# Four small products on the quarters of the matrix engine, in linear attention before a gated MLP

## The chip, the cores and the metric

The program runs on one core of a Trainium2 chip. The metric is the device time of one execution in microseconds (us). Five engines take part: PE (TensorE, the matrix engine; its weight loads are shown as PEld), DVE (VectorE), ACT (ScalarE), POOL (GpSimd) and SP (SyncE, which here only issues DMAs; ACT issues some in the first microseconds).

## The reference, cut to what matters

Inputs are q, k and v of 8 batches x 8 heads x 576 positions x 64, and two weight matrices of 512 x 2048 and 2048 x 512. The weights arrive in 64-bit floats, the rest in 32-bit floats.

```python
q_s = softmax(q, axis=-1)                 # over the 64 of a head
k_s = softmax(k, axis=2)                  # over the 576 positions
kv  = einsum('bhsd,bhse->bhde', k_s, v)   # one 64 x 64 matrix per head
x   = einsum('bhsd,bhde->bhse', q_s, kv)  # then (batch*position) x 512
h   = x @ w_in
out = (h * cos(h)) @ w_out
```

## The kernel before, in words

Positions: of the 576 of a batch, 512 are worked on with that batch, and the last 64 of every batch are collected through `x_left` in DRAM into a ninth block of 512 rows. There are thus nine blocks of 512 rows for the MLP.

The MLP. The 2048 middle columns are cut into 16 slices of 128. A unit is one slice of one block: four matrix products into a bank `h` (L1073 or L1081), the gate h*cos(h) on ACT and DVE (L1106 to L1121), and four products into four banks `acc` (L1159 or L1166). In the first units the operands stay plain 32-bit (L1073, L1159); later each operand is split into a high and a low part and three products in a faster format stand for one (L1081, L1166). Blocks 0 and 1 are taken in turn by eight slices each, then blocks 2 to 4, and the last four blocks in two pairs that share products (L1453). Weights are turned from 64-bit to 32-bit floats by two steps of ACT and two of DVE each (L556, L561, L567, L578).

Attention for one batch. Heads are taken in pairs p of neighbours, 2p and 2p+1, because two heads of 64 fill 128 partitions. `k_exps` does the softmax of k on DVE, POOL and ACT. `k_steps` multiplies k by v (L760): for each pair ten products, five chunks of positions for two heads, one head to the upper and one to the lower 64 partitions of the output bank, so each uses a half of PE's columns; then `kv_f32` (L783) copies the two 64 x 64 results onto the diagonal of a 128 x 128 matrix `kvw` which POOL has filled with zeros (L778). `q_steps` does the softmax of q. For batch 0's first two pairs (`alone`) its exponentials go row by row on ACT (L821), eighteen instructions with their sums, in two parts. `x_steps` brings q to head-dimension-first form: in batches 0 and 1 by PE transposes (L902, L906), in the later ones by DVE block transposes and a trip through DRAM (`q_rows`). Then `x_mm` (L923) multiplies, for one pair, the 128 x 128 matrix by q in two halves of 288 positions, into two banks. ACT copies 512 of the 576 positions as high part (L933) and the other 64 as rows for `x_left` (L936); DVE makes the low part. In batch 0 the copy is plain (`x_whole`), and ACT does all of it.

A 32-bit product is two records on PE in the profile (two weight loads, two MATMULs).

PSUM has eight banks: two `h`, four `acc`, two `att`. The attention takes `att` in turn after the start.

The order. Each step is added to a `Plan` with its engine, a cost, what it reads and writes and a due time (`CFG` holds the numbers that set these); the list `ORDER` then gives the order in which all steps are issued. An engine works through its own steps in that order and waits at each for what it needs. PE also gets products of zeros (`warm_up` L1647, `fill` L736) in the start.

The first loads are listed in `CFG["seq"]`: q, k and v of batch 0 by pairs of heads (two DMAs each), with the first weights among them, on the queues of SP and ACT.

Of the kernel before, what the change touches and what calls it, by code (L numbers as in the profile page):

```python
# [29 lines left out]
    XV=(),  # L30
    early=1,
# [4 lines left out]
    fill_kv=((0, 0), (0, 1), (0, 2), (0, 3)),  # L36
# [5 lines left out]
    t0=33.71,  # L42
    unit=5.32,
    att0=dict(k=(-11.28, 5.44), kv=(18.78, -0.31), q=(5.83, 11.45), qt=(12.05, 4.95), x=(9.45, -8.71)),
# [3 lines left out]
    bus=dict(k=1.15, q=1.4, v=1.2, i=2.0, o=1.32),  # L48
    slow=1.3,
# [312 lines left out]
def linear_attention_then_cos_gated_mlp(  # L362
# [58 lines left out]
    def v_parts(t):  # L421
        return (
            t[:, 0 : CM * WV].rearrange("p (x w) -> p x w", w=WV),
            t[:, CM * WV : VW].rearrange("p (h w) -> p h w", w=WL),
        )
# [228 lines left out]
    def load_v(b, p, due, seq=(), eng="SP"):  # L654
# [21 lines left out]
        if own:  # L676
            plan.add("DVE", 0.45, frame, writes=place, due=due)
# [1054 lines left out]
```

## Time and profile before

| | |
|---|---|
| time, median of 3 runs | 872.33 us (871.9 to 872.65) |
| the profiled execution, span from its first to its last instruction | 871.6 us |
| median time less that span | 0.7 us |
| mean granted TensorE clock | 0.991 |
| PE, PEld, DVE, ACT, POOL busy | 98%, 79%, 70%, 61%, 9% |

The profile is of one execution. The granted clock is a share of full speed: 1.00 is the 2.4 GHz level, 0.50 the 1.2 GHz level. In a timeline row "x40" is the number of records merged, and a duration ends with the last record's own modelled end, so the time that a run of records takes from its neighbours is read from start to start.

### The profile page before, as it was taken

The page shows a single profiled execution, that of the slowest core. Times are in us where ns is not written, and L with a number is a line of the kernel's source. Part 1 is how long each engine was busy: PE and PEld are TensorE (multiplying, and loading weights), DVE is VectorE, ACT ScalarE, POOL GpSimd, SP SyncE. Part 2 cuts the span into 40 slices and gives each one's busy share as a digit, 9 for nine tenths or more (in the row PEclk, how much of TensorE's full clock was granted, in tenths as well). Part 3 has the DMA queues.
Part 4 walks back from the last instruction along what each step waited for, and adds up shares of the span by engine and source line. Part 5 has one row for each costly group of instructions (what it writes and reads, how often), then busy time and mean ns, then how long its engine had stood idle before and what let it go on. Part 6 is the DMA issues. An engine that isn't in the chain of part 4 may idle for free.

```text
span 871.6 us, 12196 instructions
## 1 busy us (share of the span) xinstructions
PE 855.9 (98%) x4224; PEld 687.8 (79%) x4224; DVE 605.7 (70%) x976; ACT 533.3 (61%) x913; POOL 76.6 (9%) x149
## 2 busy tenths in 40 slices
PE   6999999999999999999999999999999999999997
PEld 5754678888888888888888888888888888888886
DVE  5799899987676676585698988774547736454542
ACT  5898898646555656755774776664546635353441
POOL 1110100010001001001001002111100201111000
PEclk8899999999999999999999999999999999999999
DMA  9945495237943442463478727875423726243123
GB/s 232 341 118 157 152 261 170 78 77 232 285 128 98 103 105 72 106 155 104 126 195 261 229 86 209 213 205 159 135 85 109 215 78 193 85 151 91 37 54 91
DMA packets 151996, 130.30 MB, mean 150 GB/s; under 512 B 65920, under 2 KB 125312, under 8 KB 151936
## 3 DMA queue, kind: packets, MB, share of 16 engines
q1 hardware_dynamic: 136208, 98.24, 39.8%
q0 software_dynamic: 13312, 29.36, 11.9%
q10 hardware_dynamic: 2416, 1.93, 0.8%
q8 instruction: 33, 0.54, 0.3%
q14 instruction: 27, 0.22, 0.1%
HBM read 89.92 MB, written 39.58 MB: 149 GB/s over the span
## 4 chain that ended last, share of the span: by engine, by line
PE 96%; DMA 1%; DVE 1%; SPq 1%; ACT 0%; issue 0%
PE acc L1166 43%; PE h L1081 22%; PE z L1453 10%; PE a L1453 8%; PE x L923 4%; PE h L1073 3%; PE acc L1159 2%; PE kv L760 2%; DMA q<-in_q_dram 1%; PE qt L736 1%; DMA raw_o<-in_moe_w_out_dram 1%; PE acc L736 0%; PE qt L902 0%; PE kv L736 0%; SPq L647 0%; DVE k L713 0%
## 5 line engine op out<-in xcount | busy, mean ns | idle before, releaser
L1081 PE MATMUL h<-x,w_i 128*128 128x512 f32 x864 | 208.8, 392 | 1.3 <-DVE kt L1121 1.3
L1081 PEld LDWEIGHTS h<-x,w_i 128*128 128x128 f32 x864 | 162.0, 188 | 36.0 <-DVE kt L1121 1.5
L1166 PE MATMUL acc<-w_o,ghi 128*128 128x512 f32 x592 | 188.5, 399 | 0.0
L1166 PEld LDWEIGHTS acc<-w_o,ghi 128*128 128x128 f32 x592 | 110.6, 188 | 24.3
L1166 PE MATMUL acc<-w_o,glo 128*128 128x512 f32 x296 | 115.6, 391 | 0.0
L1453 PE MATMUL z<-xs,s 128*128 128x512 f32 x384 | 96.7, 391 | 0.0
L1106 ACT ACTIVATE kt<-h 128x512 int32<-128x512 f32 x80 | 47.6, 596 | 75.6 <-PE h L1081 72.1
L1453 PEld LDWEIGHTS z<-xs,s 128*128 128x128 f32 x384 | 72.1, 188 | 15.2
L1110 DVE SCALAR_TENSOR_TENSOR kt<-kt,h 128x512 f32<-128x512 int32 x80 | 54.7, 684 | 40.1 <-ACT kt L1106 39.9
L1453 PE MATMUL a<-xs,s 128*128 128x512 f32 x288 | 73.4, 390 | 0.0
L1137 ACT CAST ghi<-kt 128x512 fp32r<-128x512 f32 x74 | 45.6, 620 | 38.9 <-PE acc L1166 33.6
L1166 PEld LDWEIGHTS acc<-w_o,glo 128*128 128x128 f32 x296 | 55.5, 188 | 11.9
L1453 PEld LDWEIGHTS a<-xs,s 128*128 128x128 f32 x288 | 54.0, 188 | 11.3
L1121 DVE TENSOR_TENSOR kt<-kt,h 128x512 f32<-128x512 f32 x74 | 50.4, 680 | 16.8 <-ACT kt L1116 16.3
L1116 ACT ACTIVATE kt<-kt 128x512 f32<-128x512 f32 x80 | 50.6, 632 | 16.6 <-DVE kt L1110 16.0
L1141 DVE TENSOR_TENSOR glo<-kt,ghi 128x512 fp32r<-128x512 f32 x74 | 50.6, 688 | 14.0 <-ACT ghi L1137 13.5
L1474 DVE TENSOR_TENSOR c<-a,c 128x512 f32<-128x512 f32 x32 | 22.1, 691 | 26.8 <-PE a L1453 19.5
L923 PE MATMUL x<-qf,kvw 128*128 128x288 f32 x128 | 38.6, 407 | 0.0
L1427 POOL DMA_DIRECT2D s<-w_sums x32 | 20.2, 630 | 168.1 <-PE a L1453 116.3
L1116 ACT ACT_TABLE_LOAD x27 | 34.6, 1283 | 0.5
L706 POOL PARTITION_ALL_REDUCE m<-m x32 | 24.8, 809 | 77.8 <-DVE m L700 69.0
L1467 ACT COPY c<-z 128x512 f32<-128x512 f32 x32 | 18.8, 586 | 19.9 <-PE z L1453 19.7
(638 smaller groups left out, 1474.4 us busy)
## 6 DMA issues: line engine op xcount, KB each, us to landing
s<-w_sums POOLq DMA_DIRECT2D x32, 512.0 KB, 4.1
q<-in_q_dram SPq DMA_DIRECT2D x32, 256.0 KB, 3.9
raw_o<-in_moe_w_out_dram SPq DMA_DIRECT2D x16, 512.0 KB, 7.1
s<-w_own POOLq DMA_DIRECT2D x16, 512.0 KB, 4.5
raw_i<-in_moe_w_in_dram SPq DMA_DIRECT2D x15, 512.0 KB, 6.4
v_sb<-in_v_dram SPq DMA_DIRECT2D x29, 256.0 KB, 3.6
k<-in_k_dram SPq DMA_DIRECT2D x14, 512.0 KB, 4.6
qf<-q_rows SPq DMA_DIRECT2D x24, 288.0 KB, 3.6
```

What stands on the lines that cost most here:

```text
L706: nc.gpsimd.partition_all_reduce(T["m", b, p0][:, hs].rearrange("p h d -> p (h d)"), T["m1", b, p0][:, hs].rearrange("p h d -> p (h d)"), ...
L923: nc.tensor.matmul(t[:, 0:HALF], T["kv", b, p], T["qf", b, p][:, cs], start=True, stop=True)
L1073: nc.tensor.matmul(o, T["wc", "i", f][:, 0, cs], T["whole"][:, c], start=(c == 0), stop=(c == KC - 1),)
L1081: nc.tensor.matmul(o, a, x, start=(c == 0 and n == 0), stop=(c == KC - 1 and n == 2))
L1106: nc.scalar.activation(t.bitcast(I32), src(), AF.Identity, bias=0.25, scale=1.0 / TWO_PI)
L1110: nc.vector.scalar_tensor_tensor(t, t.bitcast(I32), -TWO_PI, src(), op0=ALU.mult, op1=ALU.add)
L1116: nc.scalar.activation(t, t, AF.Sin, bias=0.5 * math.pi)
L1121: nc.vector.tensor_mul(o, t, src())
L1137: nc.scalar.copy(t, T["g", u])
L1141: nc.vector.tensor_sub(t, T["g", u], T["gh", u].bitcast(F32))
L1166: nc.tensor.matmul(T["acc", j], a[:, js], w, start=(first and n == 0), stop=(last and n == 2))
L1453: nc.tensor.matmul(o, a, x, start=(first and c == 0 and m == 0), stop=(c == 1 and m == 2), skip_group_check=not first,)
```

## The change

Heads are paired two apart: of the four heads 4a to 4a+3, pair 2a+i holds heads 4a+i and 4a+i+2 (h = 0 and 1). The kv results are kept as 128 x 64 (head h on partitions 64h to 64h+63) with no zeros around them and one copy per pair (L783's two become one; POOL's memset goes). x of two pairs is four products of 64 x 64 weights by 512 positions, each with 64 rows and 64 columns of PE of its own, into two banks that then hold two heads each; the leftover 64 positions of all four pairs are kept apart (`ql`, `q_left`) and are eight products of 64 positions in two further banks, with one row store per batch. In batch 0 the four copies of x are shared between ACT and DVE (`XV=(1, 3)`).

The first loads of k, q and v go by four heads (k one DMA of 512 KB and one of 64 KB; q four DMAs; v two, or four where the two standing tiles take it). In batch 0 the k steps go by four heads as in the other batches, and the first maximum of q is one instruction over all rows. `early` goes from 1 to 2: the first two units' products wait for each quarter of x by itself. Two products of zeros less (`fill_kv`). All due times of the start, load costs and the whole `ORDER` are new.

The core of the diff (the order list, load helpers, the q rows in DRAM and renamings are left out):

```diff
-    XV=(),
-    early=1,
+    XV=(1, 3),
+    early=2,
...
-    fill_kv=((0, 0), (0, 1), (0, 2), (0, 3)),
+    fill_kv=((0, 0), (0, 1)),
...
     seq=[
-        ("q", 0, "SP"), ("k", 0, "ACT"), ("q", 1, "SP"), ("i", 0, "ACT"), ("k", 1, "ACT"), ("v", 0, "SP"),
-        ("q", 2, "SP"), ("v", 1, "ACT"), ("q", 3, "SP"), ("k", 2, "SP"), ("k", 3, "SP"), ("v", 2, "SP"), ("v", 3, "SP"),
-        ("i", 1, "SP"), ("o", 0, "SP"),
+        ("k", 0, "SP"), ("q", 0, "ACT"), ("v", 0, "SP"), ("k", 1, "ACT"), ("i", 0, "SP"), ("q", 1, "SP"),
+        ("v", 1, "SP"), ("i", 1, "SP"), ("o", 0, "SP"),
     ],
...
+    def pair_of(x, b, a, i):
+        return x[b].rearrange("(a h i) s d -> a i h s d", h=2, i=2)[a, i]
...
                         nc.tensor.matmul(
-                            x[h * D : (h + 1) * D, a : a + vt.shape[1]], t[:, h, c, :], vt,
+                            x[h * D : (h + 1) * D, to : to + vt.shape[1]], t[:, i + 2 * h, c, :], vt,
                             start=(c == CM), stop=(c == CM - 1),
                         )
...
         def kv_f32(i):
-            for h in range(2):
-                rows = slice(h * D, (h + 1) * D)
-                nc.scalar.activation(
-                    T["kv", b, ps_[i]][rows, rows], T["kvp", b, ps_[0]][rows, 2 * P * i + 1 : 2 * P * i + D + 1],
-                    AF.Copy, scale=T["r", b, ps_[0]][rows, i : i + 1],
-                )
+            t = T["kv", b, 2 * a + i] = sbt([P, D], F32, kvws[i], f"kvw_{b}_{2 * a + i}")
+            nc.scalar.activation(
+                t, T["kvp", b, a][:, 2 * P * i + 1 : 2 * P * i + D + 1], AF.Copy, scale=T["r", b, a][:, i : i + 1],
+            )
...
-        def x_mm(i):
-            t = T["xp", b, p, i] = bank(xo[i], f"x{i}_{b}_{p}")
-            cs = slice(i * HALF, (i + 1) * HALF)
-            nc.tensor.matmul(t[:, 0:HALF], T["kv", b, p], T["qf", b, p][:, cs], start=True, stop=True)
...
+        def quarters_of(banks, cols, moving, a):
+            for h, i in ((0, 0), (1, 1), (0, 1), (1, 0)):
+                rows, to = slice(h * D, (h + 1) * D), slice(i * D, (i + 1) * D)
+                nc.tensor.matmul(
+                    banks[h][to, cols], T["kv", b, 2 * a + i][rows], moving(2 * a + i)[rows], start=True, stop=True,
+                )
+
+        def x_mm(a, xo):
+            banks = [bank(o, f"x_{b}_{2 * a + h}") for h, o in enumerate(xo)]
+            for h in range(2):
+                T["xp", b, 2 * a + h] = banks[h]
+            quarters_of(banks, slice(0, NM), lambda p: T["qf", b, p], a)
+
+        def x_mm_left(xo):
+            banks = T["xlp", b] = [bank(o, f"xl{h}_{b}") for h, o in enumerate(xo)]
+            for a in range(2):
+                quarters_of(banks, slice(a * NL, (a + 1) * NL), lambda p: T["ql", b][:, p], a)
...
+        def x_hi(c, slot, own):
...
+            t = T["whole"][:, c] if whole else T["x", b, c][:, 0]
+            (nc.vector.tensor_copy if own else nc.scalar.copy)(t, T["xp", b, c])
```

The new list begins, for the engines that the prediction follows, with these steps of batch 0 (read off the list by counting the steps in the order in which they are added). PE: products of zeros and `warm_up`, k times v of heads 0 to 3, the transposes of pairs 1 and 0, zeros, `x_mm` of the first four heads, k times v of heads 4 to 7, zeros, the transposes of pair 2, of the leftover and of pair 3, zeros, the first product of unit 0, `x_mm` of the last four heads, the second product, the leftover products, and the other products of units 0 and 1 in turn. ACT: the DMAs of q and k, eighteen row exponentials of q, the exponential of k (heads 0 to 3), two weight steps, the copies of pairs 1 and 0, the exponential of q (pairs 2, 3), the kv copies, the exponential of k (heads 4 to 7), the copy of x. DVE: the maximum of q, the maxima of k, then the sums' reciprocals, the subtractions and products of both in turn.

## Rows read from the trace of the kernel before

**Rows 1.** Page, part 1: busy us (share of the span) x instructions.

```profile
PE 855.9 (98%) x4224; PEld 687.8 (79%) x4224; DVE 605.7 (70%) x976; ACT 533.3 (61%) x913; POOL 76.6 (9%) x149
```

**Rows 2.** Windows: each engine's busy us by stretch, then PEclk, DMA share, GB/s.

```profile
0.00:10.00 10.00, 7.76 (x29) 6.59 (x30) 3.97 (x30) 3.52 (x15) 2.27 (x12) 1.00 0.84 201
...
20.00:35.00 15.00, 14.34 (x119) 12.88 (x120) 13.85 (x32) 12.63 (x32) 2.55 (x5) 0.69 1.10 335
35.00:40.00 5.00, 5.00 (x25) 3.56 (x24) 1.38 (x2) 4.13 (x12) 0.71 (x3) 1.00 1.10 335
40.00:60.00 20.00, 20.00 (x102) 10.84 (x101) 19.02 (x32) 19.34 (x32) 3.26 (x4) 1.00 0.60 181
60.00:80.00 20.00, 20.00 (x92) 10.01 (x91) 18.18 (x27) 17.77 (x33) 0.20 (x1) 1.00 0.38 99
80.00:100.00 20.00, 20.00 (x66) 11.25 (x65) 18.31 (x32) 17.86 (x35) 2.40 (x6) 1.00 0.54 158
100.00:112.00 12.00, 11.75 (x119) 9.37 (x117) 10.95 (x20) 11.64 (x19) 1.59 (x3) 1.00 0.70 204
112.00:150.00 38.00, 36.92 (x163) 30.54 (x164) 35.56 (x48) 35.18 (x51) 0.31 (x1) 1.00 0.80 231
...
200.00:560.00 360.00, 360.00 (x1912) 295.32 (x1911) 263.38 (x423) 227.82 (x366) 27.63 (x56) 1.00 0.58 160
```

**Rows 3.** Timeline of PE: start us, us, operation, records [idle before, releaser].

```profile
15.72 1.35 PE L760 MATMUL kv<-v_sb,k 128*64 128x66 f32 x20 [3.36 <-issue]
20.00 1.36 PE L760 MATMUL kv<-v_sb,k 128*64 128x66 f32 x20 [2.92 <-ACT k L719]
...
34.74 1.02 PE L1073 MATMUL h<-x_whole,room_i 128*128 128x512 f32 x2
...
39.73 1.02 PE L1073 MATMUL h<-x_whole,room_i 128*128 128x512 f32 x2
...
113.08 3.01 PE L1081 MATMUL h<-x,w_i 128*128 128x512 f32 x12 [1.33 <-DVE kt L1121]
```

**Rows 4.** Timeline of PE: records of x and of plain 32-bit products.

```profile
80.13 3.60 PE L1073 MATMUL h<-x_whole,room_i 128*128 128x512 f32 x8
83.56 1.13 PE L923 MATMUL x<-qf,kvw 128*128 128x288 f32 x4
84.53 3.60 PE L1159 MATMUL acc<-room_o,g 128*128 128x512 f32 x8
```

**Rows 5.** Timeline of PE: one k-times-v step and its neighbours.

```profile
204.14 1.99 PE L1081 MATMUL h<-x,w_i 128*128 128x512 f32 x8
206.06 1.39 PE L760 MATMUL kv<-v_sb,k 128*64 128x66 f32 x40
207.37 0.73 PE L1166 MATMUL acc<-w_o,ghi 128*128 128x512 f32 x2
207.94 0.39 PE L1166 MATMUL acc<-w_o,glo 128*128 128x512 f32 x1
208.17 0.62 PE L1166 MATMUL acc<-w_o,ghi 128*128 128x512 f32 x2
208.64 0.40 PE L1166 MATMUL acc<-w_o,glo 128*128 128x512 f32 x1
```

**Rows 6.** Lines of ACT by shape: count | busy us, mean ns | idle before, releaser.

```profile
L783 ACT ACTIVATE kvw<-kv,r 64x64 f32<-64x64 f32 x64 | 19.6, 307 | 4.0 <-DVE r L774 3.3
...
L719 ACT ACTIVATE k<-k 128x1280 f32<-128x1280 f32 x14 | 17.8, 1275 | 0.1
L851 ACT ACTIVATE q<-q 128x1152 f32<-128x1152 f32 x15 | 17.5, 1167 | 0.1
...
L821 ACT ACTIVATE q<-q,qm 128x64 f32<-128x64 f32 x18 | 6.0, 336 | 0.0
```

**Rows 7.** Timeline of DVE in the start.

```profile
5.77 0.69 DVE L842 TENSOR_REDUCE qm<-q 128x8 f32<-128x512 f32 x1 [2.09 <-DMA q<-in_q_dram]
...
17.09 1.35 DVE L837 TENSOR_REDUCE qm<-q 128x18 f32<-128x1152 f32 x1 [3.08 <-ACT q L821]
```

More of the change, by code (lines that the diff above doesn't have):

```diff
@@ L434, in v_frame @@
         return t
-    NV = 2
-    v_sb = [v_frame(vp.tile([P, VW], F32, name=f"v_sb{i}")) for i in range(NV)]
+    v_sb = [v_frame(vp.tile([P, VW], F32, name=f"v_sb{i}"), 2) for i in range(2)]
     w_in = w_in.bitcast(U32)
@@ L654, in load_v @@
-    def load_v(b, p, due, seq=(), eng="SP"):
-        q_of = nc.scalar if eng == "ACT" else nc.sync
-        own = b == 0 and p >= NV
-        slot = ring("x4k") if own else None
-        place = quarters(slot) if own else [("v", p % NV)]
-        def frame():
-            T["v", b, p] = v_frame(sbt([P, VW], F32, slot, f"v_{b}_{p}"))
-        def load():
-            t = T["v", b, p] if own else v_sb[p % NV]
-            main, last = v_parts(t)
-            src = v[b, 2 * p : 2 * p + 2]
+        plan.add("POOL" if b else "DVE", 0.31, frame, writes=places, due=due)
@@ new lines, in load_k, with load_q @@
+        plan.load(CFG["bus"]["k"] * 2, load, writes=places, due=due, parts=2, eng=eng)
+        return places
+    def load_q(b, a, place, due, eng="SP"):
+        places = place if isinstance(place, list) else [(place, i) for i in (0, 1)]
+        tag = place if not isinstance(place, list) else spot(*place[0][1:])
+        def load():
+            t = T["q", b, a] = sbt([P, 9, P], F32, tag, f"q_{b}_{a}")
+            q_of = QUEUE[eng]
+            for i in range(2):
+                s2 = pair_of(q, b, a, i)
+                q_of.dma_start(
+                    t[:, NC * i : NC * i + CM, :].rearrange("p c (h d) -> p c h d", h=2),
+                    s2[:, 0:NM, :].rearrange("h (p c) d -> p c h d", c=CM),
+                )
+                q_of.dma_start(
+                    t[NL * i : NL * (i + 1), CM, :].rearrange("p (h d) -> p h d", h=2),
+                    s2[:, NM:S, :].rearrange("h p d -> p h d"),
+                )
+        plan.load(CFG["bus"]["q"] * 2, load, writes=places, due=due, parts=4, eng=eng)
+        return places
@@ L788, in k_steps @@
-        if (b, ps_[0]) in CFG["fill_kv"]:
-            fill(o, 3, ("fill", b, ps_[0]), f"kv_{b}_{ps_[0]}", o, due_kv)
-        plan.add("PE", 0.93 if n == 1 else 1.51, kv, reads=kr + vr, writes=[o], due=due_kv)
-        plan.add("DVE", 0.41 if n == 1 else 0.62, kv_inv, reads=[o], writes=[r])
-        for i in range(n):
-            plan.add("POOL", 0.14, lambda i=i: kv_frame(i), writes=[kvws[i]], due=due_kv)
-            plan.add("ACT", 0.62, lambda i=i: kv_f32(i), reads=[o, r], writes=[kvws[i]])
@@ L799, in q_steps @@
+        plan.add("DVE", 0.62, kv_inv, reads=[o], writes=[r])
+        for i in range(2):
+            plan.add("ACT", 0.31, lambda i=i: kv_f32(i), reads=[o, r], writes=[kvws[i]])
+        return kvws
+    def q_steps(b, a, qr, due):
         qm, qs = ring("qm"), ring("qs")
-        def rows():
-            return T["q", b, a].rearrange("p c (h d) -> p c h d", h=2)
-        def over_d(m):
-            return m.rearrange("p c (h o) -> p c h o", o=1).broadcast_to([P, 9, 2, D])
-        parts = ((0, 2 * CM), (2 * CM, 4 * CM + 2))
@@ L816, in q_exps, with q_exp @@
+        def q_exp():
+            t = T["q", b, a]
+            nc.scalar.activation(t, t, AF.Exp)
         def q_exps(i):
-            if i == 0:
-                T["qs", b, a] = sbt([P, 9, 2], F32, qs, f"qs_{b}_{a}")
-            t, m, o = rows_of(i), flat(T["qm", b, a], i), flat(T["qs", b, a], i)
-            for r in range(parts[i][1] - parts[i][0]):
+            t, m, o = heads(T["q", b, a]), T["qm", b, a], T["qs", b, a]
+            for r in range(parts[i].start, parts[i].stop):
                 nc.scalar.activation(
@@ L849, in q_exp, with q_norm @@
[L849 to L863 removed]
+        def q_norm(rs=slice(0, n)):
+            t = heads(T["q", b, a])[:, rs]
+            nc.vector.tensor_mul(t, t, over_d(T["qs", b, a], rs))
@@ L865, in q_steps @@
+        plan.add("DVE", 1.35, q_max, reads=qr, writes=[qm, qs] if alone else [qm], due=due)
         if alone:
-            done = [qr[:1], qr]
-            for i, n in ((0, 8), (1, 10)):
+            for i, rs in enumerate(parts):
+                m = rs.stop - rs.start
                 plan.add(
-                    "DVE", 0.07 * n + 0.1, lambda i=i: q_maxs(i), reads=done[i], writes=[(qm, i)] + [qm] * (1 - i), due=due
+                    "ACT", 0.335 * m, lambda i=i: q_exps(i), reads=[qm, qs], writes=[qr[i], (qs, i)], table="exp",
@@ L870, in q_steps @@
                 )
-                plan.add(
-                    "ACT", 0.335 * n, lambda i=i: q_exps(i), reads=[(qm, i)], writes=[*done[i], (qs, i)], table="exp"
-                )
-                plan.add("DVE", 0.42, lambda i=i: q_invs(i), reads=done[i], writes=[(qs, i)])
-                plan.add("DVE", 0.07 * n + 0.06, lambda i=i: q_norms(i), reads=[(qs, i)], writes=done[i])
+                plan.add("DVE", 0.42, lambda rs=rs: q_inv(rs), reads=[qr[i], qs], writes=[(qs, i)])
+                plan.add("DVE", 0.07 * m + 0.06, lambda rs=rs: q_norm(rs), reads=[(qs, i), qs], writes=[qr[i]])
@@ L876, in q_steps @@
             return
-        plan.add("DVE", 1.35, q_max, reads=qr, writes=[qm], due=due)
         plan.add("DVE", 1.35, q_sub, reads=[qm], writes=qr)
@@ L1007, in x_steps @@
-        if blocks:
-            qb = ring("qb")
-            old = [("x_left", i) for i in range(CFG["QD"] * NP)] if b == CFG["QD"] and p == 0 else []
-            plan.add("DVE", 0.71 if odd else 0.92, q_blocks, reads=qr, writes=[qb, *old], due=due_q)
-            qd, ql = [("qd", odd)], [("qd", odd, "left")]
-            left = [] if odd else [("qd", i, "left") for i in range(2)]
-            plan.load(1.05 if odd else 1.45, q_out, reads=[qb], writes=qd + left, parts=4 if odd else 8)
-            plan.load(0.95, q_in, reads=qd + ql, writes=[qf])
-        else:
-            if (b, p) in CFG["fill_q"]:
-                fill(o1, 4, ("fill", "q", b, p), f"qt1_{b}_{p}", o1, due_q)
-            plan.add(
-                "PE", 0.44 if odd else 0.55, q_tr, writes=[o1] if odd else [o1, o2],
-                reads=qr,
-                due=due_q,
-            )
-            if not odd:
-                plan.add("ACT", 0.23, q_side, reads=[o2], writes=[ring("ql")])
-            plan.add("ACT", 0.82, q_f32, reads=[o1, o2], writes=[qf])
@@ L1026, in x_steps @@
-        us = 0.49
-        for i in range(2):
-            plan.add("PE", us, lambda i=i: x_mm(i), reads=[qf, kvw], writes=[xo[i]], due=due_x)
-        if not keep:
-            for i in range(2):
-                plan.add("ACT", 0.4, lambda i=i: x_row(i), reads=[xo[i]], writes=[xs])
-            plan.load(0.9, put, reads=[xs], writes=[("x_main", p, b), ("x_left", p, b)], parts=2)
-            return []
-        for i, us in ((0, 0.4), (1, 0.58)):
-            xw = [("whole", p)] if whole else xr if i == 0 else xr[2:3]
-            plan.add("DVE" if own else "ACT", us, lambda i=i: x_hi(i), reads=[xo[i]], writes=xw + [xs] * i)
-            if not whole:
-                plan.add(
-                    "DVE", (0.45, 0.38)[i], lambda i=i: x_lo(i), reads=[xo[i], xr[2 * i]],
-                    writes=[xr[2 * i + 1]],
-                )
@@ new lines, in x_left_row, with put_left @@
+        def x_left_row(h):
+            if h == 0:
+                T["xl", b] = sbt([P, NP, NL], F32, xl, f"xl_{b}")
+            nc.scalar.copy(
+                T["xl", b][:, h::2], T["xlp", b][h][:, 0:P].rearrange("p (a n) -> p a n", a=2)
+            )
+        def put_left():
+            nc.sync.dma_start(
+                x_left[:, :, b * NL : (b + 1) * NL].rearrange("c p n -> p c n"), T["xl", b]
+            )
+        def x_hi(c, slot, own):
+            if whole and "whole" not in T:
+                T["whole"] = sbt([P, NP, TB], F32, "wi10", "x_whole")
+            if not whole:
+                T["x", b, c] = sbt([P, 2, TB], F32R, slot, f"x_{b}_{c}")
+            t = T["whole"][:, c] if whole else T["x", b, c][:, 0]
+            (nc.vector.tensor_copy if own else nc.scalar.copy)(t, T["xp", b, c])
@@ new lines, in x_lo, with late_hi, late_lo, late @@
+        def x_lo(c):
+            t = T["x", b, c]
+            nc.vector.tensor_sub(t[:, 1], T["xp", b, c], t[:, 0].bitcast(F32))
+        def late_hi(c, slot):
+            t = T["x", b, c] = sbt([P, 2, TB], F32R, slot, f"x_{b}_{c}")
+            nc.scalar.copy(t[:, 0], T["whole"][:, c])
+        def late_lo(c):
+            t = T["x", b, c]
+            nc.vector.tensor_sub(t[:, 1], T["whole"][:, c], t[:, 0].bitcast(F32))
+        def late(c, slot, xr):
+            plan.add("ACT", 0.62, lambda: late_hi(c, slot), reads=[("whole", c)], writes=[xr[0], xr[2]])
+            plan.add("DVE", 0.69, lambda: late_lo(c), reads=[("whole", c), xr[0]], writes=[xr[1], xr[3]])
@@ new lines, in x_row, with put @@
+        def x_row(c, xs):
+            T["xs", b, c] = sbt([P, TB], F32, xs, f"xs_{b}_{c}")
+            nc.scalar.copy(T["xs", b, c], T["xp", b, c])
+        def put(c):
+            nc.sync.dma_start(x_main[b, c], T["xs", b, c])
+        got = []
+        for a in range(2):
+            qfs = []
+            for i in range(2):
+                p = 2 * a + i
+                if blocks:
+                    qb, qf = ring("qb"), ring("row")
+                    plan.add(
+                        "DVE", 0.71 if i else 0.92, lambda p=p, qb=qb: q_blocks(p, qb), reads=qrs[a], writes=[qb],
+                        due=due_q(p),
+                    )
+                    plan.load(
+                        1.05 if i else 1.45, lambda p=p: q_out(p), reads=[qb],
+                        writes=[("qd", i)] + ([] if i else [("qdl", a)]), parts=4 if i else 8,
+                    )
+                    plan.load(0.85, lambda p=p, qf=qf: q_in(p, qf), reads=[("qd", i)], writes=[qf])
+                else:
+                    o, qf = ring(tq), ring("row")
+                    if (b, p) in CFG["fill_q"]:
+                        fill(o, 4, ("fill", "q", b, p), f"qt_{b}_{p}", o, due_q(p))
+                    plan.add("PE", 0.44, lambda p=p, o=o: q_tr(p, o), reads=qrs[a], writes=[o], due=due_q(p))
+                    plan.add("ACT", 0.59, lambda p=p, qf=qf: q_f32(p, qf), reads=[o], writes=[qf])
+                qfs.append(qf)
+            xo = [ring(tx), ring(tx)]
+            plan.add(
+                "PE", 1.15, lambda a=a, xo=xo: x_mm(a, xo), reads=[*qfs, kvw[2 * a], kvw[2 * a + 1]], writes=xo,
+                due=due_x(2 * a),
+            )
+            for h in range(2):
+                c = 2 * a + h
+                if not keep:
+                    xs = ring("row")
+                    plan.add("ACT", 0.59, lambda c=c, xs=xs: x_row(c, xs), reads=[xo[h]], writes=[xs])
+                    plan.load(0.73, lambda c=c: put(c), reads=[xs], writes=[("x_main", c, b)])
+                    continue
+                slot = ring("x4k")
+                xr = quarters(slot)
+                got += xr
+                own = whole and c in CFG["XV"]
+                xw = [("whole", c)] if whole else [xr[0], xr[2]]
+                plan.add(
+                    "DVE" if own else "ACT", 0.65 if own else 0.6, lambda c=c, slot=slot, own=own: x_hi(c, slot, own),
+                    reads=[xo[h]], writes=xw,
+                )
+                if whole:
+                    splits["x", c] = lambda c=c, slot=slot, xr=xr: late(c, slot, xr)
+                else:
+                    plan.add("DVE", 0.69, lambda c=c: x_lo(c), reads=[xo[h], xr[0]], writes=[xr[1], xr[3]])
@@ new lines, in x_steps @@
+        if blocks:
+            plan.load(0.5, q_in_left, reads=[("qdl", 0), ("qdl", 1)], writes=[ql])
+        else:
+            o = ring("att")
+            plan.add("PE", 0.25, lambda: q_tr_left(o), reads=qrs[0] + qrs[1], writes=[o], due=due_q(3))
+            plan.add("ACT", 0.35, q_left_f32, reads=[o], writes=[ql])
+        xo = [ring("att"), ring("att")]
+        plan.add("PE", 0.52, lambda: x_mm_left(xo), reads=[ql, *kvw.values()], writes=xo, due=due_x(3))
+        for h in range(2):
+            plan.add("ACT", 0.28, lambda h=h: x_left_row(h), reads=[xo[h]], writes=[xl])
@@ L1051, in linear_attention_then_cos_gated_mlp @@
+        plan.load(0.5, put_left, reads=[xl], writes=[("x_left", p, b) for p in range(NP)])
+        return got
     FH = CFG["FH"]
```

407 lines of the change are left out of this document (156 added, 251 removed), and 293 rows, old and new, of the table ORDER.

## The prediction

> **What bounds the kernel now.** I read the page's busy shares first: PE is busy for 98% of the span, DVE for 70%, ACT for 61% [rows 1]. A share over the whole span hides stages, so the windows come next. From 200 to 560 us PE is busy for all of the 360 us while DVE works 263 and ACT 228 [rows 2]: here a microsecond less on PE is a microsecond less in the end, and nothing else is near. The start is another matter. The timeline of PE has idle stretches of 3.36 and 2.92 us ahead of the first two k-times-v steps; the first product of unit 0 begins at 34.74 us and its third, which needs the third quarter of x, only at 39.73 [rows 3]. Between 20 and 112 us DVE works 13.85 + 1.38 + 19.02 + 18.18 + 18.31 + 10.95 = 81.7 of 92 us and ACT 83.4 [rows 2], and just behind that PE waits 1.33 us for DVE [rows 3]. So there are three stages: a start bound by the chain from loads through ACT and DVE, a stretch to about 150 us in which PE, DVE and ACT are all nearly full (112 to 150 us: 36.9, 35.6 and 35.2 of 38), and the rest, bound by PE.
>
> **The change on PE, batches 1 to 7.** Removed: eight products of 288 columns per batch. Two of them take 84.53 - 83.56 = 0.97 us from start to start [rows 4], 0.485 each, 3.88 us per batch. A record of 288 columns is then 0.2425 us, 0.842 ns per column; a record of 512 columns is (83.56 - 80.13) / 8 = 0.429 us [rows 4].
>
> Added: two groups of four products of 512 columns (8 records, 3.43 us if they ran one by one) and one group of eight products of 64 columns (16 records, 0.86 us). No row of before has products with 64 rows of their own. The nearest is k times v, where two products have 64 columns of PE each. I take its step between full-width neighbours [rows 5]: eight records from 204.14 at 0.23 us (the step from 207.94 to 208.17) end at 205.98; the step starts at 206.06; the next work starts at 207.37, and its first two records take 0.57 us instead of 0.47 (208.17 to 208.64). That makes 0.08 + 1.31 + 0.10 = 1.49 us. Its 40 records of 65 columns would be 2.19 us one by one and 1.09 us two abreast. Thus two products do run side by side, and going to small products and back costs about 0.40 us.
>
> With four abreast a group of 512 columns is 3.43 / 4 + 0.40 = 1.26 us, the leftover group 0.86 / 4 + 0.40 = 0.62, a batch 2 x 1.26 + 0.62 = 3.14 us: 0.74 us less, 5.2 us in seven batches. The bounds: four abreast without the 0.40, 1.94 us per batch, 13.6 less in seven; two abreast, as the row has it, 2 x 2.12 + 0.83 = 5.07, 8.3 more; one by one, 2 x 3.83 + 1.26 = 8.92, 35 more. I take four abreast with the full 0.40, since the four quarters share neither rows and columns both nor a bank half, and because k times v reaches the whole of what its two column halves allow.
>
> What a rule makes of it: the Trainium skill, "TensorE: Matmul & The Clock Gate", Part 3, says that MATMULs start and end in program order without exception. Its table of measured gains has 3.07 times for four row tiles, by which I estimate 1.12 us plus the 0.40 for a group of 512; a batch would then be some 0.5 us dearer than in my sum. The first of the two would hurt more here, because each 32-bit product is two records on the same quarter; that case is a rival below, worked out from rows. Rows 5 can't settle it: in strict order 40 records would take 21 record times, 1.15 us against 1.09, which is within what I can read.
>
> **The other edits, at nothing.** The kv copies go from 64 to 32 of 0.307 us [rows 6], 9.8 us less on ACT over the run; POOL's zeros go; the copies and subtractions of x become one of 512 columns each instead of two. In the later batches this is under PE's cover, since DVE and ACT idle there by a quarter or more [rows 2]. If the cover fails, as before 150 us, they can only help. A group of four now waits at once for two `att` banks, two q rows and two kv copies, and everything on PE queues behind it. In before no such wait is seen in 360 us [rows 2]; I take none, and at most a copy and a subtraction for one group, 1.17 + 0.69 us by the longer ACT row and the 512-column DVE row [rows 6, 7]. SP issues four q DMAs in a row where it had two and two; the DMA engines are at 0.58 of their time from 200 to 560 us [rows 2], and what stands behind on SP (v, weights, rows of x) is fetched ahead, so nothing. The transposes of batches 0 and 1 stay 18 a batch. The two fills of zeros that go lay in PE's idle time of the start. The end of the run isn't touched.
>
> **The start.** 2.0 MB landed in the first ten microseconds (201 GB/s) [rows 2]. q and k of four heads are 1.18 MB and v's 0.59 share the engines with them, so I put q's last part at about 8.5 us, where before a first pair's part was there at 5.77 [rows 7]. Then, in the order read from the list: the maximum of q 1.35 us by the same shape at 17.09 [rows 7], to 9.9; eighteen row exponentials 6.0 [rows 6], to 15.9; k's exponential 1.28, to 17.2; k times v of four heads, 1.5 to 2.6 us by the clock level, to about 19. Before, the second pair's was done at 20.00 + 1.36 = 21.4 [rows 3]. From there DVE sets the pace: two steps of 1.35 for the second q with the first one's last product between them, to 20; ACT's exponential 1.17 and the copies ahead of the first x, to 22.7; that x to 24.5. DVE meanwhile has the k subtraction, sum, reciprocal and product of the second q, to about 26.5; transposes, two copies, the second x, to 30. The first product of unit 0 comes at about 28 us instead of 34.74, the third at about 31 instead of 39.73.
>
> These 7 to 9 us are not all kept. Work on DVE before 112 us doesn't shrink (the changes there are under 1 us), it idles for only 92 - 81.7 = 10.3 us between 20 and 112, and PE already waits for it there. What PE gains is what DVE can be moved forward. I take half of that idle time, 5 us. The ends: 0.5, if DVE gets no further than the work it saves, and 8.5, if its early start carries through.
>
> **The sum.** 871.6 - 5.2 - 5.0 = 861.4 us of span. The median of the runs is 0.7 above the span of the profiled run; that stays: 862.
>
> **Rivals.**
> 1. The start's gain is lost to DVE and ACT. For it: 95% of both from 40 to 60 us [rows 2]. Against it: DVE is idle for 3.6 of the 5 us from 35 on, behind the late x. 871.6 - 0.5 - 5.2 + 0.7 = 866.6. Chance 0.16.
> 2. Slower: no more than two records run abreast, in every group of four. In strict record order the second record of each product waits for its first, and the next product's first starts with it: five record times, 5 x 0.429 = 2.15 us plus 0.40, and 9 x 0.054 + 0.40 = 0.89 for the leftover: 5.99 us per batch against 3.88, 14.8 more; with plain pairs 8.3 more. 871.6 - 5.0 + 8.3 to 14.8 + 0.7 = 875.6 to 882. It decides from 3.88 + 5.0 / 7 = 4.6 us per batch on. For it: rows 5 show two, not four, and it is the skill's order rule. Against it: the four differ in rows as well. Chance 0.17.
> 3. The quarters run one by one, so the change doesn't do what it says: 871.6 - 5.0 + 35 + 0.7 = 902. The pair of [rows 5] speaks against it. 0.02.
> 4. Both terms are too small: 8.5 us of the start kept and 0.2 per change of width instead of 0.40 (1.34 us per batch, 9.4 in seven): 854. 0.09.
> 5. The new list leaves PE waits, at one group in two for half of the 1.9 us above: some 10 groups, 6 to 8 us: 868 to 870. For it: every step is listed anew, and two banks are wanted at once. Against it: the old list leaves none from 200 us on. 0.06.
>
> **How the numbers follow.** The forecast has the remaining 0.50, with 856 to 867 as its own range (0.5 us either way per batch in x, 3.5 in seven, and 2 us in the start). A measurement of this kernel tells 0.2%, 1.7 us, from no change. Faster: the forecast, rivals 1 and 4, and most of 5, 0.80; within: 0.02; slower: rivals 2 and 3, 0.18. A range of 853.5 to 870.5 leaves out rivals 2 and 3 and little else.
>
> **What would show it.** In the new profile a group of x of 8 records takes about 1.26 us from start to start of its neighbours (2.1 to 2.6 is rival 2, 3.8 rival 3), and the leftover group 0.6. The first unit's first product begins near 28 us, the third near 31; the first split product (L1081 before) begins about 5 us earlier than before. If it begins within 1 us of before while unit 0 is early, and PE's waits name DVE or ACT before 150 us, it is rival 1. PE idle beyond 150 us with `att` or a copy as the releaser is rival 5. The prediction is wrong at its root if the two x terms and the start don't add up to the change in span, above all if products that weren't touched take other durations.

## The result and the profile after

The changed kernel takes 863.29 us (median of four runs, 861.98 to 864.71) against 872.42 us for the kernel before: a ratio of 0.9895, with a 95% interval of 0.9881 to 0.9909. The forecast was 862.0. Its profiled run has a span of 860.4 us and took 862.21 us; the span is 11.2 us shorter than that of before, the medians differ by 9.1. The difference is in which runs were profiled: every recorded run of either kernel takes 1.7 to 1.8 us more than its own span, so before's 871.6 belongs to a run about 1.1 us longer than that kernel's median, and the 860.4 to one 1.1 us shorter than the median of after. What is read below from this pair of traces adds up to 11.2 us, of which 2.1 are scatter.

Part 1 of the page after (busy us, share of the span, instructions) answers to [rows 1]:

```profile
PE 844.9 (98%) x4340; PEld 664.6 (77%) x4340; DVE 600.3 (70%) x941; ACT 491.9 (57%) x819; POOL 71.4 (8%) x117
```

PE lost 11.0 us of work, about as much as the span, though it has 116 records more. ACT lost 41 us and DVE 5; shares of the whole span don't tell what that was worth, so the next view is where PE was busy. Windows of the kernel after, with the columns of [rows 2]:

```profile
16.00:20.00 4.00, 0.10 (x2) 0.10 (x4) 3.96 (x7) 4.00 (x19) 0.70 (x1) 0.59 1.17 296
20.00:24.00 4.00, 3.97 (x48) 3.61 (x48) 3.33 (x7) 1.57 (x3) 1.01 (x2) 0.56 0.96 289
24.00:30.00 6.00, 5.36 (x73) 4.36 (x74) 5.43 (x8) 4.97 (x9) 0.31 (x1) 1.00 0.54 176
...
112.00:150.00 38.00, 38.00 (x236) 31.25 (x235) 35.04 (x43) 31.66 (x41) 0.00 (x0) 1.00 0.53 158
...
200.00:560.00 360.00, 358.47 (x1997) 286.19 (x1996) 268.61 (x426) 201.84 (x317) 25.91 (x41) 1.00 0.59 165
```

From 112 to 150 us, where PE, DVE and ACT were all nearly full before, PE now has no gap. From 200 to 560 us it idles for 1.5 us. The granted clock is at 0.56 to 0.59 from 16 to 24 us, near the lower of its two levels (1.2 of 2.4 GHz); it falls while PE stands still (0.10 us busy from 16 to 20 us). The kernel before was held down in its start too (0.69 from 20 to 35 us [rows 2]), and longer: where after is at 1.00 again from 24 us on, the same window of before has 0.55.

```profile
24.00:30.00 6.00, 6.00 (x29) 5.79 (x28) 5.93 (x13) 3.98 (x11) 1.76 (x3) 0.55 1.10 344
```

The start on PE (start us, us, operation, records, idle before and releaser), beside [rows 3] and [rows 4]:

```profile
19.90 2.44 PE L760 MATMUL kv<-v,k 128*64 128x66 f32 x40 [5.91 <-ACT k L722]
...
31.94 1.02 PE L1058 MATMUL h<-x_whole,room_i 128*128 128x512 f32 x2
32.89 1.09 PE L913 MATMUL x<-qf,kvw 64*64 64x512 f32 x8
33.91 1.13 PE L1058 MATMUL h<-x_whole,room_i 128*128 128x512 f32 x2
34.97 0.46 PE L913 MATMUL xl<-ql,kvw 64*64 64x64 f32 x16
35.36 2.84 PE L1058 MATMUL h<-x_whole,room_i 128*128 128x512 f32 x6
```

Two things are read here. First, the price of x. A group of four products takes 33.91 - 32.89 = 1.02 us from start to start. The two plain records before it take 0.95 us to the next start, and the two between the groups 1.06, where two records cost 2 x 0.429 = 0.86: so 0.09 us goes ahead of a group and 0.10 behind one, and a group costs about 1.22 us in all. The leftover group, 0.39 from start to start, costs about 0.59 with the same two edges. A batch is 2 x 1.22 + 0.59 = 3.03 us, where before's was 3.88 by [rows 4]. Second, the start: unit 0's first product begins 2.8 us earlier than before and its third 4.4 us earlier, not 7 to 9.

Both prices of x are from rows between plain products. Most groups stand between split products, where a record takes 0.227 us, and there the kernel before often issued its two halves of 288 positions, two records each, apart. Its timeline:

```profile
196.93 0.65 PE L923 MATMUL x<-qf,kvw 128*128 128x288 f32 x2
197.20 0.84 PE L1166 MATMUL acc<-w_o,ghi 128*128 128x512 f32 x2
197.88 0.40 PE L1166 MATMUL acc<-w_o,glo 128*128 128x512 f32 x1
```

From 196.93 to 197.88 is 0.95 us for a half and two split records: 0.50 for the half, 4.0 us for a batch. Taken in the same way, a group of the kernel after costs 1.23 there and a leftover group 0.61, 3.1 a batch. Over all groups of both traces x went from 31.9 to 24.5 us, 7.3 us less.

Why unit 0 gained no more is in the timelines of DVE and ACT:

```profile
11.23 1.35 DVE L804 TENSOR_REDUCE qm<-q 128x18 f32<-128x1152 f32 x1 [7.91 <-DMA q<-in_q_dram]
...
18.60 1.25 ACT L722 ACTIVATE k<-k 128x1280 f32<-128x1280 f32 x1
```

The first q is complete at about 11.1 us (8.5 in the forecast). The eighteen row exponentials, 6.0 us of ACT, run from 12.62 to 18.6, the exponential of k stands behind them, and PE waits 5.91 us for it. The list of what PE waited for (us in total, times, longest) holds that wait and little else:

```profile
PE kv L760 <- ACT k L722: 5.9, 1, 5.9
PE kv L739 <- DVE v L425: 2.2, 1, 2.2
PE h L1066 <- DVE kt L1106: 1.4, 2, 1.1
PE qt L739 <- ACT qf L865: 0.7, 1, 0.7
PE z L1438 <- DVE glo L1126: 0.2, 1, 0.2
```

I also summed PE's time from start to start by tile in both traces: x, its leftover and the products of the feed-forward units went from 759.2 to 751.1 us, the zeros that fill PE's gaps in the start from 20.2 to 17.5, transposes and k times v lost 0.7, plain products gained 0.6, idle time was 8.3 and is 8.2. So in this pair about 8 us came from the part with x (7.3 of it in its groups, by the count above) and 3 from the start.

### The profile page after: what moved, and what is told of

Same layout as the page of the kernel before. It is cut to its first block, busy times and chain, and to the rows that moved or that the text cites. A ratio compares the mean times of both kernels' runs of the same rounds, so it can differ in the third digit from the quotient of the medians.

```text
span 860.4 us, 12174 instructions
## 1 busy us (share of the span) xinstructions
PE 844.9 (98%) x4340; PEld 664.6 (77%) x4340; DVE 600.3 (70%) x941; ACT 491.9 (57%) x819; POOL 71.4 (8%) x117
## 4 chain that ended last, share of the span: by engine, by line
PE 92%; DMA 3%; SPq 1%; ACT 1%; DVE 1%; issue 0%; ACTq 0%; DVEq 0%
PE acc L1151 42%; PE h L1066 21%; PE z L1438 10%; PE a L1438 7%; PE h L1058 3%; PE acc L1144 2%; PE kv L760 2%; PE x L913 2%; DMA q<-in_q_dram 2%; ACT q L817 1%; DVE qm L804 0%; PE acc L739 0%; PE qt L861 0%; PE xl L913 0%; SPq L635 0%
## 5 line engine op out<-in xcount | busy, mean ns | idle before, releaser
L1151 PE MATMUL acc<-w_o,ghi 128*128 128x512 f32 x592 | 184.7, 393 | 0.0
L1101 ACT ACTIVATE kt<-kt 128x512 f32<-128x512 f32 x80 | 50.4, 632 | 32.8 <-DVE kt L1095 31.9
L1122 ACT CAST ghi<-kt 128x512 fp32r<-128x512 f32 x74 | 45.1, 616 | 31.9 <-PE acc L1151 25.8
L1438 PEld LDWEIGHTS a<-xs,s 128*128 128x128 f32 x288 | 54.0, 188 | 11.2
L804 DVE TENSOR_REDUCE qm<-q 128x18 f32<-128x1152 f32 x16 | 21.6, 1351 | 20.0 <-DMA q<-in_q_dram 19.8
L1412 POOL DMA_DIRECT2D s<-w_own x32 | 20.2, 633 | 117.3 <-PE a L1438 80.1
```

The lines of the kernel that those rows point to most:

```text
L1101: nc.scalar.activation(t, t, AF.Sin, bias=0.5 * math.pi)
L1122: nc.scalar.copy(t, T["g", u])
L1151: nc.tensor.matmul(T["acc", j], a[:, js], w, start=(first and n == 0), stop=(last and n == 2))
L1412: nc.gpsimd.dma_start(t, src)
L1438: nc.tensor.matmul(o, a, x, start=(first and c == 0 and m == 0), stop=(c == 1 and m == 2), skip_group_check=not first,)
```

## The experiments

Each kernel is the changed one with the edit shown, unless it is said otherwise. Its ratio is to the kernel before on the same chip, whose median was 872.32 us in the first four and 872.74 in the others.

**Full width with everything else of the change.** Neighbouring heads are paired again and the four quarters of a group become two products on all of PE, against block-diagonal tiles whose zeros are written once. Loads, list of steps and leftover group stay.

```diff
         def quarters_of(banks, cols, moving, a):
-            for h, i in ((0, 0), (1, 1), (0, 1), (1, 0)):
-                rows, to = slice(h * D, (h + 1) * D), slice(i * D, (i + 1) * D)
-                nc.tensor.matmul(
-                    banks[h][to, cols], T["kv", b, 2 * a + i][rows], moving(2 * a + i)[rows], start=True, stop=True,
-                )
+            for i in range(2):
+                p = 2 * a + i
+                nc.tensor.matmul(banks[i][:, cols], T["kv", b, p], moving(p), start=True, stop=True)
```

> The changed kernel with its own order of steps and loads, but heads paired with their neighbours again, the kv results on the diagonal of 128 x 128 tiles (zeroed once at the start, two copies per pair on ACT, six tiles instead of eight), and x of two pairs as two products of full width and 512 columns (1.72 us by the row of 0.429 us per record) and four of 64 columns for the leftover (0.43). Theory A, the quarters are worth their price on PE: a batch pays 2 x 1.72 + 0.43 = 3.87 us instead of 2 x 1.22 + 0.59 = 3.03, 0.84 more, 6.7 in eight batches: 870 us against 863.3. Theory B, the gain is the start's and the new list's, and the quarters only fill time that PE would wait in anyway: 863 to 866.

873.44 us, ratio 1.001 (1.0001 to 1.002): without the quarters the whole gain is gone, and 10.2 us were lost against the changed kernel, more than any theory gave. PE's timeline of this kernel, and the row of its weight loads (PEld), show the rest:

```profile
67.02 3.60 PE L1149 MATMUL acc<-room_o,g 128*128 128x512 f32 x8
70.46 1.88 PE L920 MATMUL x<-qf,kvz 128*128 128x512 f32 x4
72.17 3.60 PE L1063 MATMUL h<-x_whole,room_i 128*128 128x512 f32 x8
...
114.66 1.00 PE L920 MATMUL xl<-ql,kvz 128*128 128x64 f32 x8
115.47 3.00 PE L1071 MATMUL h<-x,w_i 128*128 128x512 f32 x12
...
114.44 1.08 PEld L920 LDWEIGHTS xl<-ql,kvz 128*128 128x128 f32 x8
```

A full-width group takes 72.17 - 70.46 = 1.71 us, and nothing is lost at its edges (67.02 to 70.46 is eight records at 0.43). The leftover group takes 115.47 - 114.66 = 0.81 us, 0.101 a record where 64 columns are worth 0.429 / 8 = 0.054, and what stands behind it takes 0.10 us longer. From its second record on the products start 0.11 us apart, and so do the weight loads, back to back over 1.08 us; I take it from this that the loads set the pace, which no run tests. A batch is 2 x 1.71 + 0.91 = 4.33 us: 1.30 more than with quarters, 10.4 us in eight batches, against the 10.2 measured. Against the 3.9 to 4.0 us per batch of before it is 0.3 to 0.4 more, some 3 in eight, yet the kernel is only 1.1 slower (873.44 against 872.32): **the other parts of the change are worth about 2 us, the quarters the rest.** Little of these 2 us is an earlier unit 0, which begins at 34.33 us in this kernel's trace, 0.4 before that of the first; PE's idle time is 1.4 us less.

**Another order of the four quarters.** Products with the same half of the moving rows follow each other.

```diff
-            for h, i in ((0, 0), (1, 1), (0, 1), (1, 0)):
+            for h, i in ((0, 0), (0, 1), (1, 0), (1, 1)):
```

> The changed kernel with the four products of a group in the order (0,0), (0,1), (1,0), (1,1) (row half, column half), so that neighbours in the list share their rows. Theory A, four records of different quarters start within some 20 ns and the order doesn't matter: 863 us, 1.02 us from start to start of a group of 8 records. Theory B, a product must differ from its neighbour in rows as well to run beside it: the group takes 0.43 to 0.86 us more, 7 to 14 us in 16 groups, 870 to 877.

862.48 us (0.9888, 0.9872 to 0.9905): no difference from the changed kernel's 863.29 or from its repetition below, and in the trace a group takes 1.02 us from start to start as there (67.18 to 68.20). This other order of the four doesn't change their overlap.

**The first q on two queues.** Half of its loads are issued on SP's queue, ahead of k and v: the edit changes the queue of that half and its place among the loads at once.

```diff
-            q_of = QUEUE[eng]
             for i in range(2):
+                q_of = QUEUE["SP" if i else eng]
                 s2 = pair_of(q, b, a, i)
```

> The changed kernel with the second pair of each q load issued by SP, so that the first q of batch 0 goes out on both queues ahead of k and v. In the changed kernel q's last part landed at 11.1 us, behind v's 576 KB, and the first k times v began at 19.9. Theory A, the start is the chain from that landing through the eighteen row exponentials: q lands at about 6.5, the table load ends at 8 to 9, the first k times v begins near 16, and 2 to 4 us of it reach the end: 859 to 861. Theory B, as in the prediction's first rival, DVE and ACT take it back before 150 us: the first k times v begins near 16 too, but PE waits for DVE grow and the time is 862.5 to 864.

860.83 us (0.9863, 0.9842 to 0.9884). Its timeline, DVE and PE:

```profile
6.29 1.35 DVE L804 TENSOR_REDUCE qm<-q 128x18 f32<-128x1152 f32 x1 [2.97 <-DMA q<-in_q_dram]
10.10 0.69 DVE L694 TENSOR_TENSOR mt<-k 128x512 f32<-128x512 f32 x1 [2.46 <-DMA k<-in_k_dram]
...
16.90 2.27 PE L760 MATMUL kv<-v,k 128*64 128x66 f32 x40 [2.71 <-ACT k L722]
...
28.85 1.02 PE L1058 MATMUL h<-x_whole,room_i 128*128 128x512 f32 x2
...
678.45 1.63 PE L1438 MATMUL z<-xs,s 128*128 128x512 f32 x6 [0.21 <-DMA s<-w_sums]
```

q is there 5 us earlier. In the changed kernel that half had been issued from 2.25 us on, behind the first half on ACT's queue, with k and v issued beside it on SP's from 0.73 to 2.9; here it is issued at 0.73 us, ahead of k. So it was where the load stood that made q late; how much of that was the queue and how much the order isn't told apart. Now k is late, issued at 2.54 us instead of 0.73, and the gain on PE is 3.1 us at unit 0. Compared instruction by instruction, PE's list stays 2.7 to 3.5 us ahead of the changed kernel's until about 680 us; between there and 716 us, where a wait of 0.21 for the sums' weights shows, the lead falls to 2.1, and so it ends. So in this pair of traces two thirds of the start's gain are carried through all that DVE and ACT have to do behind it.

**More zeros in the start.** The products that keep PE busy before the first k times v go from 14 to 26.

```diff
-    warm=14,
+    warm=26,
```

> The changed kernel with 26 products of zeros in the warm-up instead of 14, about 5 us more of PE work at the full clock in the 5.9 us in which PE waits for the first k times v. In the profiled run the clock fell to 0.50 at 16.7 us for 6.8 us; by the mean clocks of the four runs (0.991 and 0.993 against 0.995 and 0.996) two of them had twice that, and were 2.4 us longer. Theory A, the low clock at the start costs time on the way to the first unit: no stretch at 0.50 before the first unit, all runs within 0.5 us of each other, 859.5 to 861.5. Theory B, the start is set by ACT and DVE and PE's clock there is hidden: 862 to 864, and the spread stays.

862.16 us (0.988, 0.9863 to 0.9896), one microsecond under the changed kernel's first measurement and 0.3 under its second, which is within the scatter. In the timeline of PE the step of 40 records takes 1.39 us, not 2.44, so the clock stood at its upper level (1.00 from 14 to 24 us), and unit 0 came 1.4 us earlier:

```profile
20.08 1.39 PE L760 MATMUL kv<-v,k 128*64 128x66 f32 x40 [1.06 <-ACT k L722]
...
30.56 1.02 PE L1058 MATMUL h<-x_whole,room_i 128*128 128x512 f32 x2
...
680.14 1.63 PE L1438 MATMUL z<-xs,s 128*128 128x512 f32 x6 [0.36 <-DMA s<-w_sums]
```

Of the 1.4 us, 1.3 are left at 680 us; they are lost there and at 717 us, by waits that the trace shows at 0.36 and 0.33 us, and the profiled run ends 0.15 us ahead.

**The changed kernel once more,** without an edit, for a measure of the scatter.

> The changed kernel itself once more, on the chip of the three below. 862 to 865 us; runs of both lengths, 862.1 and 864.5, are expected again if the length of the low clock in the start differs from run to run.

862.45 us (0.989, 0.9874 to 0.9907), four runs from 861.46 to 864.05. Their spans are 859.9, 861.4, 862.3 and 859.7 us at mean clocks of 0.994, 0.996, 0.995 and 0.996: the length doesn't follow the clock of the run.

**Both edits of the start, with 20 zeros.**

```diff
-    warm=14,
+    warm=20,
...
-            q_of = QUEUE[eng]
             for i in range(2):
+                q_of = QUEUE["SP" if i else eng]
```

> The changed kernel with the first q on both queues and 20 warm-up products instead of 14. With the first alone, q landed at 6.29 us, the first k times v began at 16.90 behind k's landing at 10.08, PE was idle for 2.71 us before it, the clock was low in part of 15 to 25 us, and the time was 860.83 with runs from 858.7 to 863.0. Theory A, the start's chain runs over PE too when its clock is low: no low clock before the first unit, the first unit's first product at 28 us instead of 28.9 and 31.9, runs within 1 us, 858 to 860. Theory B, what PE gains in the start is lost again to waits later (the zeros alone gave 1.4 us at the first unit and 0.15 at the end of the profiled run, lost at 680 and 717 us in waits of the shared products for their weight loads): 860 to 861.5.

859.95 us (0.9855, 0.9838 to 0.9871), 0.9 under q's kernel alone, which is within the scatter. The timeline of PE shows that at unit 0 the two gains don't add up:

```profile
18.24 1.39 PE L760 MATMUL kv<-v,k 128*64 128x66 f32 x40 [1.27 <-ACT k L722]
...
28.83 1.02 PE L1058 MATMUL h<-x_whole,room_i 128*128 128x512 f32 x2
```

The first k times v runs at the upper clock but begins 1.3 us later than with q alone (18.24 against 16.90), and unit 0 begins at 28.83 us where q alone had 28.85. Later 1.09 us is lost in a single wait:

```profile
252.10 0.74 PE L1151 MATMUL acc<-w_o,ghi 128*128 128x512 f32 x2 [1.09 <-DVE o L1193]
```

**Each group of x twice.** The four products of 512 columns are issued a second time with the same operands into the same banks, so that the price of the columns and the price of going to quarters and back come apart.

```diff
-            quarters_of(banks, slice(0, NM), lambda p: T["qf", b, p], a)
+            for _ in range(2):
+                quarters_of(banks, slice(0, NM), lambda p: T["qf", b, p], a)
```

> The changed kernel with the four products of 512 columns of each group done twice, one set behind the other, so 16 records in a group. Theory A, the sum of the prediction, 0.86 us of columns four abreast and 0.40 once per group for the change of width: 16 x 0.86 = 13.7 us more, 876 to 877.5, no second pause inside a group. Theory B, the pause belongs to each set of four: 16 x 1.2 = 19 more, 882.

875.06 us (1.0031, 1.0018 to 1.0044), 12.6 us more than the repetition's 862.45. PE's timeline:

```profile
34.22 1.95 PE L913 MATMUL x<-qf,kvw 64*64 64x512 f32 x16
36.10 1.13 PE L1059 MATMUL h<-x_whole,room_i 128*128 128x512 f32 x2
```

A doubled group takes 36.10 - 34.22 = 1.88 us from start to start, 0.86 more than a single one, and 0.86 is two full records: eight more records in the time of two. Over the run x grew by 13.65 us, 16 x 0.853. So the columns run four abreast without loss, and what is left of a single group, 1.22 - 0.85 = 0.37 us, is paid once for the visit to the quarters however many products it holds.

**The first k ahead.** The first q on both queues, the second k behind v on SP's queue, 18 zeros, and in the list of steps v's load (two steps) ahead of the second k's, and the subtraction of the first k's maximum, with the two POOL steps that it needs, ahead of the second k's maximum. What each of these edits gives by itself isn't measured.

```diff
-    warm=14,
+    warm=18,
...
-        ("k", 0, "SP"), ("q", 0, "ACT"), ("v", 0, "SP"), ("k", 1, "ACT"), ("i", 0, "SP"), ("q", 1, "SP"),
+        ("k", 0, "SP"), ("q", 0, "ACT"), ("v", 0, "SP"), ("k", 1, "SP"), ("i", 0, "SP"), ("q", 1, "SP"),
...
-    2, 9, 12, 46, 7, 8, 4, 5, 13, 10, 6, 51, 17, 18, 14, 11, 15, 16, 27, 28, 29, 39, 52, 53, 21, 54, 19, 30, 131,
+    2, 9, 12, 46, 7, 8, 4, 5, 10, 13, 6, 51, 17, 18, 11, 14, 15, 16, 27, 28, 29, 30, 31, 32, 39, 52, 53, 21, 54, 19, 131,
```

> The changed kernel with the first q on both queues, k of heads 4 to 7 behind v of heads 0 to 3 on SP instead of on ACT's queue, the subtraction of the first k ahead of the second k's maximum on DVE, and 18 warm-up products. Theory A, the start is one chain and now its exponentials end it: k lands at about 8, its subtraction is done before the eighteen exponentials end at 13.6, the first k times v begins at about 15 instead of 16.9 and 19.9, the first unit about 27: 857 to 859. Theory B, the next link, q of heads 4 to 7 and k of heads 4 to 7 on DVE, sets the second x anyway: the first unit comes no earlier than 28.5 and the time is that of the kernel with q on both queues and zeros.

**858.12 us (0.9836, 0.9809 to 0.9863): faster than both kernels,** 4.3 us under the repetition. Its timeline, DVE and PE:

```profile
6.09 1.35 DVE L776 TENSOR_REDUCE qm<-q 128x18 f32<-128x1152 f32 x1 [2.77 <-DMA q<-in_q_dram]
7.83 0.69 DVE L666 TENSOR_TENSOR mt<-k 128x512 f32<-128x512 f32 x1 [0.39 <-DMA k<-in_k_dram]
...
16.07 1.39 PE L732 MATMUL kv<-v,k 128*64 128x66 f32 x40
...
26.53 1.02 PE L1030 MATMUL h<-x_whole,room_i 128*128 128x512 f32 x2
```

The first k times v follows without a gap and at the upper clock, and unit 0 begins 5.4 us before that of the changed kernel, 8.2 before the first. Of PE's waits these remain:

```profile
PE kv L711 <- DVE v L397: 2.2, 1, 2.2
PE qt L711 <- ACT qf L837: 0.7, 1, 0.7
PE acc L1123 <- DVE o L1165: 0.3, 1, 0.3
PE xl L885 <- ACT ql L846: 0.3, 1, 0.3
```

The profiled run is 5.4 us ahead of the changed kernel's at unit 0, 4.9 from 40 to 250 us and 6.0 at its end. The rise comes from delays in the changed kernel's trace that this one lacks, 1.8 us together, of which a wait of 1.1 at 368 us is one; so some 4 of the 5.4 us were kept. The run is one of the two short ones of its four; the medians differ by 4.3 to 5.2.

## Why the prediction came out right, and where it didn't

**x on the quarters** held in mechanism and nearly in size. The forecast had 3.43 / 4 + 0.40 = 1.26 us for a group, 0.62 for the leftover and 3.14 for a batch; the trace has 1.22, 0.59 and 3.03 between plain products, 1.23, 0.61 and 3.1 between split ones. The 0.40, taken from k times v, is 0.37 here, and the doubled groups show that it is what the forecast took it for, a price per visit. What it had too small was the price before: its 3.88 us a batch, from rows between plain products, is 4.0 between split ones. Counted over all groups seven batches give 6.5 us where 5.2 stood, and batch 0, which the forecast had inside the start, another 0.85.

**The start** was over-sized: 5.0 us taken, about 2 in the medians by the full-width kernel and 3 in the profiled pair. Two steps of it failed. "I put q's last part at about 8.5 us" came from an average rate, 2.0 MB in ten microseconds; where the last part stood in its queue, and what the other queue carried, was not asked. It landed at 11.1, and at 6.3 with half of it ahead of k on the other queue. The idle time that this opened also cost clock: the 40 records of k times v took 2.44 us instead of 1.39. And "What PE gains is what DVE can be moved forward" was no bound. DVE works 82.2 us between 20 and 112 us, as much as before; yet PE is without a gap from 35 to 200 us, and the kernels whose unit 0 began 3.1 and 5.4 us earlier were still 3.0 and 4.9 us ahead at 250 us. Windows of the kernel after:

```profile
20.00:112.00 92.00, 91.33 (x510) 54.98 (x511) 82.24 (x131) 75.06 (x127) 9.31 (x13) 0.98 0.64 195
35.00:200.00 165.00, 165.00 (x821) 115.15 (x821) 145.50 (x213) 128.47 (x197) 8.40 (x13) 1.00 0.54 161
```

The wait of 1.33 us in [rows 3] on which I rested that limit was a single one, not a queue of work.

**The edits taken at nothing** cost nothing that shows on PE: its waits name neither a bank of `att` nor a copy of kv. The kv copies on ACT went to 32 of twice the width, 9.5 us for 19.6 in [rows 6]:

```profile
L774 ACT ACTIVATE kvw<-kv,r 128x64 f32<-128x64 f32 x32 | 9.5, 309 | 4.2 <-DVE r L770 4.2
```

**The rivals.** The first had the start's gain lost to DVE and ACT, with a first split product no earlier. It begins at 91.0 us against 104.7, but that mark was badly chosen, since the new list also puts it earlier among the other products; the carried gains of the two start kernels are what speaks against this rival. The second, two records abreast in strict order, wanted 2.55 us for a group; 1.22 was measured. In the records behind the row at 32.89 us four starts lie at 32.894, 32.900, 32.908 and 32.914, and four more from 33.374 to 33.394: four abreast, then four. By the order rule in the Trainium skill, "TensorE: Matmul & The Clock Gate", Part 3, as I had applied it to pairs of records, this couldn't be; the measurement decides, and since the trace doesn't say which record belongs to which product, it stays open whether the records are issued in another order than I took or their starts overlap regardless of it. The third (one by one) is out by the same rows. Of the fourth, the small price per visit was not there (0.37, not 0.2), and the large gain of the start was to be had only with other loads. The fifth had waits behind the new list; there are 1.4 us of them from 200 us on, for `kt`, not the 6 to 8.

**The sum** came within 1.3 us of the median in part because the two errors have opposite signs: x gave 6.5 for 5.2 and batch 0 0.85, the start some 2 for 5. That they nearly cancel is luck. The 0.7 us was misread: a run stands 1.8 us over its own span in both kernels, and 0.7 was left because before's profiled run was 1.1 us longer than the median one. The sum isn't touched by it, since 871.6 + 0.7 is the median before, less the two gains; by the medians x with 7.3 and the start with about 2 make up the 9.1.

What stays open is the scatter. Runs of one changed kernel differ by 1.5 to 4.6 us: the four of the best kernel are 855.95, 856.15, 860.09 and 860.51, at clocks of 1.0, 1.0, 0.998 and 0.999. Waits of up to 1.1 us appear in one trace and not in another (at 252, 680 and 717 us above), and gains end in them; whether they explain the scatter would need profiles of both kinds of run.

## What to carry to other kernels

Small products that use a quarter of PE are worth grouping, four to a visit and as many sets in one visit as the banks allow: here the columns ran four abreast, and the price of 0.37 us was per visit. Read when a load lands from its place in its queue and from what the other queues carry, not from the mean rate. And where PE is the bound, microseconds won at its start can be carried far: 3.1, 1.4, 3.1 and 5.4 us at unit 0 (q, zeros, both, the first k ahead) were 2.1, 0.15, 2.0 and 6.0 at the end of the profiled runs, where the repetition, without an edit, is 0.4 ahead; what was lost went mostly at a few single waits. The share of busy time of the engines beside PE is not a wait.

## What the runs showed of the hardware that I had not expected

Full-width 32-bit products of 64 columns run at 0.101 us a record, nearly twice the 0.054 that their columns are worth, with a weight load to each at the same pace; on quarters 16 records of the same columns took 0.39 us, 0.024 each. And moving half of a load of 576 KB to the head of the other queue brought its end from 11.1 to 6.3 us, with the same bytes to load in all; what DVE then waited for was the first k, behind that half on its queue, which came at 10.1 us. In the last kernel this k, issued at 2.54 us in both, came at 7.8: there the second k no longer loads beside it on ACT's queue but stands behind v on SP's.
